# Attention plus expert layer on one Trainium2 core: a ninth shared pair of chunks, other step orders, and the output's rows copied in DRAM

## The chip, the cores and the metric

The kernel runs on one core of one Trainium2 chip. The metric is device microseconds of one execution. Before the change three runs took 1771.78 to 1775.19 us, with a median of 1773.52 us.

The engines have the names of the profile: PE is TensorE (matrix multiply), DVE is VectorE, ACT is ScalarE, POOL is GpSimd, and SP is SyncE, which here only issues DMAs.

## The reference

Eight batches of 2496 tokens with 256 features pass through an attention without softmax, and every token then goes to at most one of eight experts.

```python
scores = (1 / S) * (z @ z.T)             # z: 8 x 2496 x 64; the same z on both sides
attn = np.maximum(scores, 0.0) ** 2      # symmetric, since scores is
x = u * (attn @ v)                       # u, v: 8 x 2496 x 256
# mixture of experts over the 19968 rows of x
do_compute = x @ w_skip > 0              # the other rows go out as x
e = argmax(x @ w_gate); g = softmax(x @ w_gate)[e]
out = x + g * (relu(x @ w1[e]) @ w2[e])  # w1: 8 x 256 x 1024, w2: 8 x 1024 x 256
```

## The kernel before, in words

**Chunks and steps.** Each batch has five chunks of queries, numbered 0 to 4: four of 512 queries and a last one of 448. For each chunk the kernel walks over the keys in ten steps of 256 keys, p = 0 to 9. Keys 2p and 2p+1 (in units of 128) form step p, and p // 2 is the number of the group of 512 keys, so that group j holds the same tokens as chunk j. `steps` lists all 400 pairs (chunk, p) in the order that the table `ORDER` gives for each chunk number; chunk 0 of batch 0 goes straight through. Below, "step k" is the k-th step of a chunk in that order, from 0, and "p" is the number of the keys.

**What one step does.** PE multiplies z by z for 256 keys (`scores`, L263): six matmuls on half the array's rows, three passes of two that run side by side. ACT takes the relu from PSUM (L304) and squares it (L305) into a tile `r`. `r` is then split into a high part `ah` (a cast, L327, on ACT or DVE) and a low part `al` (a subtraction on DVE, L331), so that PE can multiply in its reduced fp32 format without losing digits. PE then accumulates v against `ah` and `al` (`attend`, L358): 12 matmuls for each half d of the features, 24 for a step (18 for p = 9), each reading 512 or 448 columns, again two side by side.

**Shared weights.** Because the weights are symmetric, the block (chunk c, key group j) is the transpose of (chunk j, key group c). The table `PAIRS` says which blocks are computed once: for a pair (c, j), chunk c computes the two steps of group j, DVE transposes `r` in blocks (`keep`, L280), and SP writes the result to a DRAM buffer `kept` (L705, four DMAs for a pair, at most four in a step). Chunk j later reads it back (`recall`, L292, four DMAs for a step) and has no scores, relu or square for those two steps. Chunk 4 has 448 queries in another layout than the others; for a recalled step of it the cast and the subtraction are each made in three pieces. Batch 0 uses only the pairs whose first chunk isn't 0.

**Which engine casts.** `on_act` puts the cast on ACT for the steps of a pair, on both sides, and for the steps listed in `EXTRA` for that chunk; the other casts are on DVE.

**Order of the work.** The order on each engine is the order of the program, written out by hand. In step k the program first issues the recall for five steps ahead, then makes the scores and weights for two steps ahead, then multiplies step k. The second half of the features (d = 1) lags: step 0 and step 8 multiply d = 0 alone, step 1 also does d = 1 of steps 0 and 1, and step 9 does d = 1 of steps 8 and 9. In step 9 the program does this, in order:

1. d = 0 of step 9;
2. the split of the next chunk's step 0 (cast and subtraction), ahead of `part` when the cast is on DVE, behind `part` when it is on ACT;
3. `part(0, ...)`: ACT copies one half of the accumulators out (L386), DVE adds the other (L388);
4. scores, relu and square of the next chunk's step 1;
5. d = 1 of steps 8 and 9;
6. `part(1, 1)`, an ACT copy that waits for the end of d = 1;
7. the cast of the next chunk's step 1, then the DVE add, then the subtraction, and then the multiplication by u (`mul`, L391).

If the next chunk's step 1 is a recalled one, its cast and subtraction come ahead of point 6 instead.

**After a chunk.** Two steps after the end come the router's matmuls (`gates`) and the first of two transposes of the rows on DVE (L395), then the second; `store` (L404) then writes the rows from the tile `xrow` with four DMAs into `xr` (in DRAM, read later by the experts), and a step later, with four more, into `out`. Each of these DMAs moves pieces of 256 bytes. After every other chunk the routing of two chunks follows on DVE: `logits` at two steps after the end, `route` and `counts` at four, `place` at six. DVE also splits the next batch's z and v as they arrive.

**Limits that matter here.** There are five `r` tiles, three each of `ah` and `al`, two of the PSUM tiles for scores, and two of the transposed tile `rt`. After the last chunk the experts run: rows are gathered from `xr` by POOL, two matrix products follow, and the results are scattered over the rows of `out` (L666).

Of the kernel before, what the change touches and what calls it, by code (L numbers as in the profile page):

```python
# [25 lines left out]

PAIRS = ((0, 1), (0, 2), (0, 3), (1, 2), (1, 3), (2, 3), (2, 4), (3, 4))
ORDER = (  # L30
# [5 lines left out]
)  # L36
EXTRA = ((8,), (3, 8), (4, 5), (6, 7), (1, 3))


C_TRI, C_REV, C_OFF, C_IDS, C_THR, C_END = 0, 128, 192, 256, 260, 270  # L40
# [7 lines left out]
def attn_moe(ctx, tc, zT, uT, v, wg, w1, w2, cst, pad, out):  # L48
# [322 lines left out]
    def finish(ci):  # L371

        b, q0, n = chunks[ci]
        t0 = b * S + q0
        xT = xTs[ci] = uts.pop(ci)

        nm = n // 32
        xrow = xp.tile([P, QC // 32, D // 4], F32, name="xrow", tag="xrow")


        e = xrow.rearrange("p a b -> p (a b)").rearrange("p (d q) -> p d q", d=2)

        def part(d, t, acc):

            if t:
                nc.scalar.copy(e[:, d, :n], acc[1][:, :n])  # L386
            else:
                nc.vector.tensor_add(e[:, d, :n], acc[0][:, :n], e[:, d, :n])  # L388

        def mul():  # L390
            nc.vector.tensor_mul(xT[:, :, :n], e[:, :, :n], xT[:, :, :n])  # L391

        def turn_rows(d):

            nc.vector.transpose(  # L395
                xrow[:, :nm, 32 * d : 32 * d + 32], xT[:, d, :n].rearrange("p (m i) -> p m i", i=32)
            )

        dsts = [xr, out]

        def store():
            dst = dsts.pop(0)
            for a in range(4):
                nc.sync.dma_start(  # L404
                    dst[t0 : t0 + n, 64 * a : 64 * a + 64].rearrange("(m i) e -> i m e", i=32),
                    xrow[32 * a : 32 * a + 32, :nm, :],
                )

        return part, mul, lambda: turn_rows(0), lambda: turn_rows(1), store
# [365 lines left out]
    for s, (ci, p) in enumerate(steps):  # L775
        b, q0, n = chunks[ci]
        k = s % NP
        step[0] = s
        ahead(s + LA + 3)
        if k == 0:  # L780
            accs[ci] = [[ps_acc.tile([P, QC], F32, name="acc", tag="acc") for _ in range(2)] for _ in range(2)]
        acc = accs[ci]
        if k < NP - 1:
            high, low = stage(s + LA)
            if k < NP - 2 or s + LA in known:
                high()
                low()
                high = low = lambda: None
            while k == NP - 3 and put_off:
                put_off.pop()()  # L790
            attend(b, n, p, 0, acc[0], *aa[s], k == 0, False)
            for t in () if k in (0, NP - 2) else (s - 1, s) if k == 1 else (s,):
                attend(b, n, steps[t][1], 1, acc[1], *aa.pop(t), t % NP == 0, False)
            rest = high, low
        else:


            part, mul, rows0, rows1, store = finish(ci)
            attend(b, n, p, 0, acc[0], *aa[s], False, True)

            high, low = rest
            if s + 1 < len(steps) and not on_act(*steps[s + 1]):
                high()
                low()
                high = low = lambda: None
            part(0, 1, acc[0])
            part(0, 0, acc[0])
            high()
            low()
            high, low = stage(s + LA)  # L810
            attend(b, n, steps[s - 1][1], 1, acc[1], *aa.pop(s - 1), False, False)
            if s + LA in known:

                high()
                low()
                high = low = lambda: None
            attend(b, n, p, 1, acc[1], *aa.pop(s), False, True)
            part(1, 1, acc[1])
            high()
            part(1, 0, acc[1])  # L820
            low()
            mul()
            accs.pop(ci)

            new.append(ci)
            if ci < NC - 1:
                after = [(rows0, 2), (rows1, 3), (store, 4), (store, 5)]
                if ci % 2 == 0:
                    gates, logits, route, counts, gate, place, put_in = routing(new)
                    after = [(gates, 2), (logits, 2), (rows0, 2), (rows1, 3), (route, 4), (counts, 4),  # L830
                             (store, 4), (gate, 5), (store, 5), (place, 6)]
                    for t in range(0, 4 * len(new), 2):
                        f = lambda put_in=put_in, t=t: put_in(t, t + 2)
                        if s + 6 + t < len(steps):
                            after.append((f, 6 + t))
                        else:
                            left.append(f)
                    new = []
                for f, k in after:
                    todo.setdefault(s + k, []).append(f)  # L840
            else:
                gates, logits, route, counts, gate, place, put_in = routing(new, False)
        for f in todo.pop(s, []):
            f()
        put_some()
# [50 lines left out]
    def add(fills, *slots):  # L896
        for k, f in slots:
            fills.setdefault(k, []).append(f)
# [4 lines left out]
    for e in range(E):  # L903
# [3 lines left out]
        for i in range(NFIX):  # L907
            fills = {}
            if e:

                add(fills, (1, rows(e, i + 3)), (3, lambda: turn_pe(pair(e, i + 1), turned(e, i + 1))))
                if e == 1 and i == 0:
                    add(fills, (0, rows(1, 2)))
                if more:
                    add(fills, (4, rows(e + 1, i)))
                if i == 0 and e + 2 < E:
                    add(fills, (6, lambda: load_ids(idts[e + 2], e + 2, 2 * NSTAT)))
                add(fills, *zip((1, 3, 5), wq[3 * i : 3 * i + 3]))
            elif i == 0:
                add(fills, (0, lambda: turn_pe(pair(0, 1), turned(0, 1))))  # L920
                add(fills, (0, gates), (0, rows0), (0, rows1), (0, store), (0, store), (1, logits), (1, route),
                    (2, counts), (2, gate), (4, end_routes), (6, end_lists))
                add(fills, *zip((0, 2), left))
            elif i == 1:
                add(fills, (1, end_counts), (3, lambda: turn_pe(pair(0, 2), turned(0, 2))), (4, rows(0, 3)), (6, rows(0, 4)))
                add(fills, *zip((1, 3, 5), wq[:3]))
            else:
                add(fills, (1, rows(1, 0)), (3, rows(0, 5)), (4, lambda: turn_pe(pair(0, 3), turned(0, 3))),
                    (5, rows(1, 1)), (6, lambda: load_ids(idts[2], 2, 2 * NSTAT)))
                add(fills, *zip((1, 2, 3, 5, 6), wq[3:]))  # L930
# [99 lines left out]
```

## Time and profile before

| | before |
|---|---|
| runs | 1771.78, 1773.52, 1775.19 us |
| the profiled execution's own time | 1774.26 us |
| its span, first to last instruction | 1772.5 us |
| TensorE clock granted | 0.998 |
| busy: PE, DVE, ACT, POOL | 1751.5, 1196.0, 1159.2, 491.4 us |
| end of the attention (last `mul`) | 1276.2 us |
| DMA bytes | 267.47 MB in 403766 packets, 205859 of them under 512 bytes |

The profile is of one execution; its time and its span differ by 1.8 us, and the execution lies 0.7 us above the median of the three runs. Busy shares are averages over two stages: the attention up to 1276 us, and the experts after it. The busy time of PE is modelled: a matmul that overlaps the one before it is counted as busy, and short waits can hide in it. They show in the distance between the starts of matmuls, which the timeline gives.

### The profile page before, as it was taken

To read this page: it belongs to the slowest core of one execution; us is meant where nothing else is said; L and a number is where in the kernel's file an instruction comes from. 1 tells how busy PE (TensorE), PEld (TensorE's weight loads), DVE (VectorE), ACT (ScalarE), POOL (GpSimd) and SP (SyncE) were. 2 spreads that over 40 slices of the span, in tenths; PEclk is the share of its full clock that TensorE was granted. 3 is DMA by queue.
4 is the path that set the end of the run, shared out by engine and by line. 5 is a ranking of instruction groups with operands and counts; after the bars stand their busy time and mean duration, and the time that the engine had idled before them with its cause. 6 is when DMAs were issued, how large, how long until landed. Compare 5 with 4: busy or idle time off the path is not lost. (4 is left out here: it accounts for less than half of the span.)

```text
span 1772.5 us, 40706 instructions
## 1 busy us (share of the span) xinstructions
PE 1751.5 (99%) x15844; PEld 1571.7 (89%) x15844; DVE 1196.0 (67%) x2113; ACT 1159.2 (65%) x1499; POOL 491.4 (28%) x483
## 2 busy tenths in 40 slices
PE   8999999999999999999999999999999999999998
PEld 6879888988888898888889888888899999999998
DVE  6878877887887787788778778867753333343332
ACT  8878877887788788778778877877533323333321
POOL 1102212211220221221122022112355546635721
PEclk9999999999999999999999999999999999999999
DMA  5576689478858947885794789579543323323210
GB/s 191 126 186 147 162 212 226 103 197 219 175 141 203 226 108 195 219 201 134 185 219 114 195 211 206 119 193 217 146 112 88 82 80 110 92 54 93 87 38 27
DMA packets 403766, 267.47 MB, mean 151 GB/s; under 512 B 205859, under 2 KB 334117, under 8 KB 403440
## 3 DMA queue, kind: packets, MB, share of 16 engines
q1 hardware_dynamic: 389440, 240.47, 55.6%
q0 software_dynamic: 13712, 22.99, 4.6%
q8 instruction: 142, 2.33, 0.6%
q14 instruction: 184, 1.51, 0.3%
q10 hardware_dynamic: 288, 0.17, 0.0%
HBM read 145.80 MB, written 118.39 MB: 149 GB/s over the span
## 5 line engine op out<-in xcount | busy, mean ns | idle before, releaser
L358 PE MATMUL acc<-ah,vh 64*128 64x512 f32 (+1 forms) x3120 | 654.6, 383 | 1.2 <-DVE ah L327 0.6
L358 PE MATMUL acc<-ah,vl 64*128 64x512 f32 (+1 forms) x3120 | 638.0, 382 | 0.0
L331 DVE TENSOR_TENSOR al<-r,ah 128x1024 fp32r<-128x1024 f32 (+3 forms) x464 | 488.4, 1068 | 185.2 <-ACT ah L327 175.4
L358 PE MATMUL acc<-al,vh 64*128 64x512 f32 (+1 forms) x3120 | 506.3, 383 | 2.2 <-DVE al L331 1.6
L517 POOL DMA_INDIRECT lst<-pair,dest x160 | 197.2, 1233 | 911.7 <-DVE dest L515 875.9
L304 ACT ACTIVATE r<-ps 128x1024 f32<-128x1024 f32 (+1 forms) x278 | 279.9, 1007 | 167.7 <-PE ps L263 158.7
L358 PEld LDWEIGHTS acc<-ah,vh 64*128 64x128 f32 x3120 | 344.6, 184 | 50.7 <-ACT ah L327 3.5
L358 PEld LDWEIGHTS acc<-ah,vl 64*128 64x128 f32 x3120 | 343.3, 184 | 41.3 <-DVE vl L120 0.3
L358 PEld LDWEIGHTS acc<-al,vh 64*128 64x128 f32 x3120 | 320.5, 184 | 53.0 <-DVE al L331 11.7
L327 ACT CAST ah<-r 128x1024 fp32r<-128x1024 f32 (+3 forms) x381 | 330.6, 892 | 55.5 <-PE acc L358 35.4
L305 ACT ACTIVATE r<-r 128x1024 f32<-128x1024 f32 (+1 forms) x278 | 290.0, 1043 | 8.8
L622 ACT ACTIVATE hh<-psh 128x512 fp32r<-128x512 f32 (+1 forms) x172 | 99.1, 584 | 287.9 <-PE psh L617 249.4
L617 PE MATMUL psh<-xt,w1h 128*128 128x256 f32 (+1 forms) x1280 | 235.3, 285 | 2.0 <-ACT xt L588 1.4
L636 PE MATMUL y<-w2t,hh 128*128 128x256 f32 x1328 | 235.5, 280 | 0.0
L623 DVE SCALAR_TENSOR_TENSOR hl<-psh,hh 128x512 fp32r<-128x512 f32 (+1 forms) x172 | 113.3, 671 | 137.5 <-ACT hh L622 134.6
L636 PEld LDWEIGHTS y<-w2t,hh 128*128 128x128 f32 x1328 | 201.8, 188 | 1.0 <-issue 0.6
L617 PEld LDWEIGHTS psh<-xt,w1h 128*128 128x128 f32 x1280 | 197.4, 189 | 2.9 <-issue 2.9
L636 PE MATMUL y<-w2t,hl 128*128 128x256 f32 x664 | 184.5, 278 | 1.3 <-DVE hl L623 1.3
L617 PE MATMUL psh<-xt,w1l 128*128 128x256 f32 (+1 forms) x640 | 182.1, 285 | 0.5 <-issue 0.5
L280 DVE STREAM_TRANSPOSE rt<-r 128x512 f32<-128x512 f32 x244 | 158.3, 686 | 0.7 <-DMA kept<-rt 0.5
L636 PEld LDWEIGHTS y<-w2t,hl 128*128 128x128 f32 x664 | 124.7, 188 | 1.7 <-DVE hl L623 1.7
L666 POOL DMA_INDIRECT out<-o,idt x77 | 76.7, 996 | 171.4 <-DVE o L665 148.6
(178 smaller groups left out, 1694.9 us busy)
## 6 DMA issues: line engine op xcount, KB each, us to landing
kept<-rt SPq DMA_DIRECT2D x244, 256.0 KB, 4.7
r<-kept SPq DMA_DIRECT2D x488, 128.0 KB, 4.5
raw<-in_v SPq DMA_DIRECT2D x80, 256.0 KB, 4.4
ut<-in_uT SPq DMA_DIRECT2D x32, 512.0 KB, 4.6
xr<-xrow SPq DMA_DIRECT2D x128, 128.0 KB, 3.2
out<-xrow SPq DMA_DIRECT2D x128, 128.0 KB, 3.0
raw<-in_w SPq DMA_DIRECT2D x64, 256.0 KB, 3.7
zf<-in_zT SPq DMA_DIRECT2D x40, 256.0 KB, 4.9
```

Source lines behind the costliest of these rows:

```text
L280: nc.vector.transpose(t[:, :, 32 * k : 32 * k + 32], r[:, x, :].rearrange("p (m i) -> p m i", i=32))
L304: nc.scalar.activation(r[:, :, :n], ps[:, :, :n], AF.Relu, scale=isc)
L305: nc.scalar.activation(r[:, :, :n], r[:, :, :n], AF.Square)
L327: (nc.scalar.copy if on_act(ci, p) else nc.vector.tensor_copy)(h_, r_)
L331: nc.vector.tensor_sub(l_, r_, f32(h_))
L358: nc.tensor.matmul(acc[t][:, :n], w[h, x, dd], a[h, x, :n], start=(first and t not in halves[:m]), stop=(last and t not in halves[m + 1 :]),)
L517: put = nc.gpsimd.indirect_dma_start(out=lst, out_offset=bass.IndirectOffsetOnAxis(ap=dest[:, t : t + 1], axis=0), in_=pair[:, t, :], in_o ...
L617: nc.tensor.matmul(ps[:, j * W : (j + 1) * W], wt[:, a, o : o + P], x[:, d, :W], start=(m == 0), stop=(m == 5),)
L622: nc.scalar.activation(hh[:, : G * W], ps[:, : G * W], AF.Relu)
L623: nc.vector.scalar_tensor_tensor(hl[:, : G * W], ps[:, : G * W], 0.0, f32(hh[:, : G * W]), op0=ALU.max, op1=ALU.subtract)
L636: nc.tensor.matmul(ys[t], h[:, tt], w2t[f][:, k, :], start=(f == 0 and m == 0 and t % 2 == 0), stop=(f == NF - 1 and m == 2), skip_group_c ...
L666: put = nc.gpsimd.indirect_dma_start(out=out, out_offset=bass.IndirectOffsetOnAxis(ap=ids[:, t, 0:1], axis=0), in_=ot, in_offset=None, bou ...
```

## The change

The pair (1, 4) joins the table, in all eight batches. Chunk 1 transposes and keeps the weights of its steps p = 8 and 9, and chunk 4 recalls them for p = 2 and 3. The order of chunk 1 changes, so that the kept groups 2, 3 and 4 each have their two steps side by side and the recalled steps p = 0 and 1 come at k = 3 and k = 6. `EXTRA` changes: in chunk 1, p = 8 leaves the list (it is in a pair now); in chunk 4, p = 0, 1 and 8 are cast on ACT in place of p = 1 and 3. `store` keeps its first part. Its second part becomes one DMA from `xr` to `out`, in 64 contiguous pieces of 7 or 8 KB, issued four steps after the first part instead of one (after the last chunk: in a later slot of the first unit of expert 0).

```diff
-PAIRS = ((0, 1), (0, 2), (0, 3), (1, 2), (1, 3), (2, 3), (2, 4), (3, 4))
+PAIRS = ((0, 1), (0, 2), (0, 3), (1, 2), (1, 3), (1, 4), (2, 3), (2, 4), (3, 4))
 ORDER = (
     (0, 1, 2, 3, 8, 4, 5, 6, 7, 9),
-    (2, 3, 0, 4, 1, 5, 8, 6, 7, 9),
+    (2, 4, 5, 0, 6, 7, 1, 8, 9, 3),
     (4, 0, 1, 6, 2, 7, 3, 8, 9, 5),
     (6, 0, 2, 1, 8, 3, 9, 4, 5, 7),
     (0, 1, 2, 3, 4, 5, 6, 7, 8, 9),
 )
-EXTRA = ((8,), (3, 8), (4, 5), (6, 7), (1, 3))
+EXTRA = ((8,), (3,), (4, 5), (6, 7), (0, 1, 8))
...
-        dsts = [xr, out]
+        stored = []
 
         def store():
-            dst = dsts.pop(0)
+            if stored:
+                to, of = (t[t0 : t0 + n, :].rearrange("(p r) d -> p (r d)", p=64) for t in (out, xr))
+                nc.sync.dma_start(to, of)
+                return
+            stored.append(True)
             for a in range(4):
                 nc.sync.dma_start(
-                    dst[t0 : t0 + n, 64 * a : 64 * a + 64].rearrange("(m i) e -> i m e", i=32),
+                    xr[t0 : t0 + n, 64 * a : 64 * a + 64].rearrange("(m i) e -> i m e", i=32),
                     xrow[32 * a : 32 * a + 32, :nm, :],
                 )
...
-                after = [(rows0, 2), (rows1, 3), (store, 4), (store, 5)]
+                after = [(rows0, 2), (rows1, 3), (store, 4), (store, 8)]
...
                     after = [(gates, 2), (logits, 2), (rows0, 2), (rows1, 3), (route, 4), (counts, 4),
-                             (store, 4), (gate, 5), (store, 5), (place, 6)]
+                             (store, 4), (gate, 5), (place, 6), (store, 8)]
...
-                add(fills, (0, gates), (0, rows0), (0, rows1), (0, store), (0, store), (1, logits), (1, route),
+                add(fills, (0, gates), (0, rows0), (0, rows1), (0, store), (3, store), (1, logits), (1, route),
```

## The prediction

> **What bounds the kernel now.** I read the page first, then the windows of the five chunks of one batch, then the timelines of PE, ACT and DVE around the steps that the change touches.
>
> ```profile
> span 1772.5 us, 40706 instructions
> PE 1751.5 (99%) x15844; PEld 1571.7 (89%) x15844; DVE 1196.0 (67%) x2113; ACT 1159.2 (65%) x1499; POOL 491.4 (28%) x483
> PEclk9999999999999999999999999999999999999999
> ```
>
> PE is busy from end to end at its full clock; no other engine is near it. The windows of chunks 1 to 4 of batch 4 say whether that holds where the change is made (columns: the stretch, then busy time and count of PE, PEld, DVE, ACT and POOL, the clock, DMA share, GB/s):
>
> ```profile
> 680.38:712.72 32.34, 32.34 (x310) 26.11 (x310) 27.33 (x58) 25.71 (x30) 5.40 (x4) 1.00 0.76 187
> 712.72:744.22 31.50, 31.40 (x274) 25.32 (x272) 22.31 (x29) 25.00 (x27) 6.74 (x6) 1.00 0.88 216
> 744.22:776.26 32.04, 31.78 (x308) 26.06 (x306) 25.33 (x52) 22.58 (x28) 5.28 (x4) 1.00 0.90 220
> 776.26:803.71 27.45, 27.45 (x270) 25.72 (x268) 23.48 (x38) 21.46 (x34) 6.33 (x8) 1.00 0.66 146
> ```
>
> In chunks 1 and 4 PE is never idle by this count, so fewer matmuls mean less time, as long as the data for the others are ready. That is the question, because each removed matmul also takes away time in which ACT and DVE prepare the next step. The page cannot answer it; the distances on the timelines can.
>
> **Term 1: the scores that go.** At the turn from chunk 3 to chunk 4 of batch 4, PE's timeline reads:
>
> ```profile
> 773.13 0.62 PE L358 MATMUL acc<-al,vh 64*128 64x512 f32 x4
> 773.58 0.36 PE L263 MATMUL ps<-zh 64*128 64x448 f32 x2
> ...
> 774.19 0.36 PE L358 MATMUL acc<-ah,vh 64*128 64x448 f32 x2
> ...
> 775.00 0.57 PE L358 MATMUL acc<-al,vh 64*128 64x448 f32 x4
> 775.41 0.36 PE L263 MATMUL ps<-zh 64*128 64x448 f32 x2
> ...
> 776.02 0.36 PE L358 MATMUL acc<-ah,vh 64*128 64x448 f32 x2
> ...
> 776.82 0.37 PE L358 MATMUL acc<-al,vh 64*128 64x448 f32 x2
> ```
>
> One step's scores take 774.19 - 773.58 = 0.61 us. Chunk 4 loses them for p = 2 and 3 in all eight batches: 16 x 0.61 = 9.8 us. The Trainium skill (TensorE: Matmul & The Clock Gate, Back-to-back issue gap) gives N/2.4 + 2.5 ns between warm matmuls; an estimate from it is 189 ns a pass, 9.1 us in all, and a sum 0.7 us smaller. The trace has the duration, so 9.8 stands.
>
> **Term 2: what the lost scores covered.** The two groups of scores above, at 773.58 and 775.41, are exactly those of p = 2 and 3. They stand between the end of chunk 3 and the first use of chunk 4's step p = 1. That step is not a recalled one, so the program casts it behind the ACT copy of chunk 3's last accumulators, and that copy waits for PE. ACT, then DVE:
>
> ```profile
> 773.79 0.59 ACT L386 COPY xrow<-acc 128x512 f32<-128x512 f32 x1 [0.84 <-PE acc L358]
> 774.27 0.94 ACT L327 CAST ah<-r 128x896 fp32r<-128x896 f32 x1
> ```
>
> ```profile
> 775.25 1.09 DVE L331 TENSOR_TENSOR al<-r,ah 128x896 fp32r<-128x896 f32 x1 [0.15 <-ACT ah L327]
> ```
>
> The chain is tied to the end of chunk 3 at 773.58: copy, cast done at 775.21, subtraction done at 776.34. PE wants `ah` at 776.02 and `al` at 776.82, so today the chain is 0.48 us early. Without the two groups PE wants `ah` at 774.80 and `al` at 775.60, both 1.22 us sooner, while the chain cannot start sooner. `ah` is then 0.41 us late and `al` 0.74 us late in all. This wait is new, on the path, and comes once in each batch: 8 x 0.74 = 5.9 us. Behind it on PE stands everything; ACT and DVE merely get ahead. The low end is 0.41 (only the cast is late): 3.3 us. The high end comes from the cast of p = 0, which the change puts on ACT ahead of this copy: 0.94 us into an idle time of 0.84, so 0.10 later, 0.84 in all, 6.7 us. I take 5.9, since each link has its row.
>
> That such a chain stops PE can be seen today at the turn from chunk 0 to chunk 1, where step 2 is recalled and only one group of scores lies between. PE, then DVE:
>
> ```profile
> 680.10 0.48 PE L358 MATMUL acc<-ah,vl 64*128 64x512 f32 x2
> 680.52 0.72 PE L358 MATMUL acc<-al,vh 64*128 64x512 f32 x4
> ```
>
> ```profile
> 679.24 1.23 DVE L331 TENSOR_TENSOR al<-r,ah 128x1024 fp32r<-128x1024 f32 x1 [0.26 <-ACT ah L327]
> ```
>
> PE starts `al` at 680.52, just after the subtraction ends at 680.47, where a start at about 680.33 was due by the pace of the rest. The page's busy count does not show this 0.2 us. In the new chunk 1 the group between moves from step 3 to step 2, so this small wait stays as it is.
>
> **Term 3: the fuller DVE in chunk 1.** Four more transposes cost DVE 4 x 0.69 = 2.7 us in each chunk 1:
>
> ```profile
> L280 DVE STREAM_TRANSPOSE rt<-r 128x512 f32<-128x512 f32 x244 | 158.3, 686 | 0.7 <-DMA kept<-rt 0.5
> ...
> L327 DVE CAST ah<-r 128x1024 fp32r<-128x1024 f32 x51 | 36.6, 718 | 17.7 <-ACT r L305 17.5
> ```
>
> One cast (of p = 9 or its successor at the chunk's end) leaves DVE, 0.7 us, so its load in chunk 1 goes from 27.3 to some 29.3 of 32.3 us. That fits on average. In even batches the routing falls there too, and the order matters. DVE in batch 4, then PE:
>
> ```profile
> 691.90 1.23 DVE L331 TENSOR_TENSOR al<-r,ah 128x1024 fp32r<-128x1024 f32 x1 [2.84 <-ACT ah L327]
> 693.05 1.30 DVE L280 STREAM_TRANSPOSE rt<-r 128x512 f32<-128x512 f32 x2
> ...
> 697.69 0.69 DVE L120 TENSOR_TENSOR vl<-raw,vh 128x512 fp32r<-128x512 f32 x1
> 698.29 2.35 DVE L331 TENSOR_TENSOR al<-r,ah 128x1024 fp32r<-128x1024 f32 x2
> ```
>
> ```profile
> 687.79 0.39 PE L263 MATMUL ps<-zqh,zh 64*128 64x512 f32 x2
> ...
> 688.47 0.39 PE L358 MATMUL acc<-ah,vh 64*128 64x512 f32 x2
> ```
>
> ```profile
> 699.76 0.62 PE L358 MATMUL acc<-al,vh 64*128 64x512 f32 x4
> ```
>
> The subtraction for k = 6 is the first of the two at 698.29, done at about 699.45; PE wants it at 699.76, 0.3 us later. In the new order k = 4 has scores, so those of k = 5 at 687.79, and the subtraction, transposes and routing behind them, come one group (688.47 - 687.79 = 0.68 us) later, while PE's own date for k = 6 stays (two groups are missing before it in both orders). 0.3 - 0.68 makes a wait of about 0.35 us in batches 2, 4 and 6: 1.1 us. The low end is 0, if the 2.84 us in which DVE idled before 691.90 take it up; the high end 0.68 in four batches, 2.7 us.
>
> **Costed at nothing.** Chunk 4's ACT and DVE lose two relus, two squares and some casts, which only adds room. The recalls and the copy go through SP and the DMA rings. DMA issues with KB each and us to landing, and the windows of chunk 4's first half:
>
> ```profile
> r<-kept SPq DMA_DIRECT2D x488, 128.0 KB, 4.5
> ...
> xr<-xrow SPq DMA_DIRECT2D x128, 128.0 KB, 3.2
> out<-xrow SPq DMA_DIRECT2D x128, 128.0 KB, 3.0
> ```
>
> ```profile
> 774.00:780.00 6.00, 6.00 (x62) 5.57 (x60) 4.79 (x7) 5.91 (x8) 1.87 (x2) 1.00 1.00 224
> 780.00:786.00 6.00, 6.00 (x64) 5.55 (x62) 6.00 (x9) 4.63 (x12) 4.46 (x7) 1.00 1.00 159
> 786.00:792.00 6.00, 6.00 (x62) 5.56 (x60) 5.01 (x12) 3.42 (x6) 0.00 (x0) 1.00 1.06 257
> 792.00:798.00 6.00, 6.00 (x62) 5.46 (x62) 4.64 (x6) 4.61 (x7) 0.00 (x0) 1.00 0.30 90
> ```
>
> The rings are full until 792 and then nearly empty. Eight recalls more (1 MB, 4.7 us at 224 GB/s) make the last ones later, and the four `out` stores that go give about half back. The cover is that a recalled step is cast two steps (2 x 2.44 us, from 774.19 to 775.41 twice for one) before its matmuls. The new wait in front of the copy holds SP's queue, with recalls and puts behind it; the `xr` stores land in 3.2 us and the copy is issued four steps, some 10 us, after them, so it finds them landed. A copy inside DRAM is not in the trace: between 3.0 us (one store) and 12 us (four in a row). It matters only at the end of the attention, where POOL's first scatter must wait for the last copy. SP, then POOL:
>
> ```profile
> 1279.67 2.00 SPq L404 DMA_DIRECT2D xr<-xrow  x4
> ```
>
> ```profile
> 1295.84 0.98 POOL L666 DMA_INDIRECT out<-o,idte  x1 [0.30 <-issue]
> ```
>
> Stores landed at about 1285 and a copy of 12 us end at 1297, at worst 1 us late; I take 0.
>
> **Sum.** -9.8 + 5.9 + 1.1 = -2.8 us against the profiled execution's 1774.26 us (span 1772.5 and 1.8 around it): 1771.5. That execution lies 0.7 us above the median of the runs, 1773.52, so the median after is 1770.7. With the ends of the terms the change lies between -6.5 and -0.4: 1767.0 to 1773.1. Runs of this kernel can tell 0.2%, 3.5 us, from no change.
>
> **The rivals.** *The saving goes through*: PE does not stop at p = 1, because what I call a chain is looser than the one execution shows. -9.8 + 1.1 gives 1764.8. For it speaks that PE counts no idle time in chunk 4; against it that the copy waited for PE and each link follows within 0.1 us. *Slower, by late recalls*: six recalled steps in a row meet full rings. If 4.7 us of delay and a landing that grows from 4.5 to 6 us exceed the cover of 4.9 by 1.3 us, eight batches pay 10.4 and the result is 1781.1. It decides from 0.35 us a batch (no gain) and from 0.8 us (slower by 0.2%). Against it: the `out` stores leave the rings, and the first two recalls come when no others are due. *Relief of the rings*: fewer small packets end the waits in chunks 2 and 3, where PE lacks 0.10 and 0.26 us; seven batches make 2.5, and 1768.2. The Trainium skill (DMA: Bandwidth & Descriptors, Specifications) asks for at least 512 bytes a piece for full rate, which the old stores miss. The trace does not bear that out here: their 128 KB land in 3.0 us, those of the recalls in 4.5.
>
> **How the numbers follow.** The forecast has 0.58: 0.40 within 0.2%, 0.16 faster, 0.02 slower. The saving that goes through has 0.17 and the relief 0.10, both faster. Late recalls have 0.15: 0.12 slower, 0.03 the same. That makes 0.43, 0.43 and 0.14. The range reaches down past the first rival, 1764.0, and up to 1776.5, into the mild part of late recalls.
>
> **What would show it.** After: no scores for p = 2 and 3 in chunk 4; PE idle for about 0.4 and then 0.3 us at the second step of chunk 4 in all batches, released by ACT's cast (L327) and DVE's subtraction (L331); a small wait at k = 6 of chunk 1 in even batches. I am wrong if PE runs through that second step, or if it waits for `r<-kept` in the middle of chunk 4.

## The result, and the profile after

The kernel after takes 1802.95 us (median of four runs, 1800.52 to 1805.44), the kernel before, run beside it, 1774.30 us (median of four). The ratio is 1.0167, with a 95% interval of 1.0154 to 1.0179: 29 us slower, where 3 us less were forecast. Two later sets of runs repeat it, with 1795.35 us against 1772.13 (1.0138, 1.0116 to 1.0159) and 1790.91 against 1773.01 (1.0111, 1.0094 to 1.0127). So from set to set the kernel after differs by up to 12 us and the kernel before by 3: a few us between runs of different sets say little. The profiled execution is the one of 1800.52 us. First its page:

```profile
span 1798.7 us, 40622 instructions
PE 1758.3 (98%) x15748; PEld 1534.9 (85%) x15748; DVE 1198.5 (67%) x2145; ACT 1161.4 (65%) x1531; POOL 501.3 (28%) x483
```

There are 96 matmuls fewer (16 groups of six), as the change says, the granted clock is 0.997, and yet PE is idle for 40 us instead of 21. The attention's last `mul` comes at 1301.5 us instead of 1276.2. So 25 of the profiled execution's 26 us are lost before the experts. The windows of chunks 1 to 4 of batch 4 in the kernel after (columns as before):

```profile
696.29:728.22 31.93, 31.59 (x302) 25.25 (x300) 27.75 (x59) 25.89 (x30) 5.59 (x4) 1.00 0.79 197
728.22:759.52 31.30, 31.20 (x272) 25.14 (x270) 22.31 (x28) 24.81 (x27) 6.55 (x6) 1.00 0.86 224
759.52:791.57 32.05, 31.50 (x300) 25.21 (x296) 24.77 (x50) 23.24 (x30) 6.20 (x4) 1.00 0.83 195
791.57:823.33 31.76, 28.99 (x264) 24.67 (x264) 22.71 (x39) 19.86 (x35) 7.33 (x8) 1.00 0.76 179
```

Chunks 1 to 3 are within half a microsecond of before. Chunk 4, which had 27.45 us without idle time, has 31.76 us, of which PE is busy for 28.99. So the loss is in chunk 4. What it waits for is in the list of waits (us in total, times, longest), first of before, then of after:

```profile
ACT ah L327 <- DMA r<-kept: 6.7, 7, 3.4
```

```profile
ACT ah L327 <- DMA r<-kept: 58.0, 31, 4.0
```

ACT's casts wait for recalled tiles 58.0 us in place of 6.7. One chunk shows how that reaches PE. ACT's timeline in chunk 4 of batch 4, after:

```profile
795.54 1.13 ACT L327 CAST ah<-r 128x384 fp32r<-128x384 f32 x3 [3.95 <-DMA r<-kept]
798.71 1.13 ACT L327 CAST ah<-r 128x384 fp32r<-128x384 f32 x3 [2.04 <-DMA r<-kept]
...
802.19 1.13 ACT L327 CAST ah<-r 128x384 fp32r<-128x384 f32 x3 [1.82 <-DMA r<-kept]
...
805.43 1.13 ACT L327 CAST ah<-r 128x384 fp32r<-128x384 f32 x3 [1.60 <-DMA r<-kept]
...
808.86 1.12 ACT L327 CAST ah<-r 128x384 fp32r<-128x384 f32 x3 [1.78 <-DMA r<-kept]
...
810.41 0.91 ACT L304 ACTIVATE r<-ps 128x896 f32<-128x896 f32 x1
...
813.71 0.91 ACT L304 ACTIVATE r<-ps 128x896 f32<-128x896 f32 x1
```

and PE's in the same stretch, the lines that carry a wait and the last scores of p = 8:

```profile
799.89 0.47 PE L358 MATMUL acc<-ah,vh 64*128 64x448 f32 x2 [0.21 <-ACT ah L327]
801.86 0.68 PE L358 MATMUL acc<-al,vh 64*128 64x448 f32 x4 [0.89 <-DVE al L331]
...
806.74 0.36 PE L263 MATMUL ps<-zh,zl 64*128 64x448 f32 x2
...
816.32 0.47 PE L358 MATMUL acc<-ah,vh 64*128 64x448 f32 x2 [1.19 <-DVE ah L327]
```

Five recalled tiles in a row (p = 3 to 7) come after ACT is ready for them. One of them, p = 4, stops PE directly, twice: by its cast at 799.89 and by its subtraction at 801.86. The second stop has another cause beside the late recall: DVE takes 2.55 us for that subtraction (from 799.26), where the next recalled tile's takes 1.18, and POOL's casts of z (L242) run beside it. At the usual pace it would have ended at 800.5, before PE asked for it at about 800.8. The largest stop, at 816, is named for DVE's cast, a step that is not recalled at all. It goes back to the same cause: the scores of p = 8 are done at 807.1, but their relu runs at 810.41, because ACT works in program order and stands until 808.86 at the cast of the last recalled tile. The relu of p = 9 follows at 813.71, behind p = 8's square and its own cast, and everything behind that is late.

To add this up I take PE's time from the first matmul of a step (d = 0) to that of the next, kernel after minus kernel before, summed over the eight batches. Idle marks alone would give too little: at 790.58 (below) the mark says 0.31 us, the starts say 0.46. In chunk 4:

| step k | 0 | 1 | 2 | 3 | 4 | 5 | 6 | 7 | 8 | 9 |
|---|---|---|---|---|---|---|---|---|---|---|
| us | -1.1 | +3.3 | 0.0 | +0.8 | +6.8 | +1.8 | +1.8 | +0.5 | +8.0 | +4.7 |

Steps 0 and 1 sum to +2.2, steps 2 to 9 to +24.4. By batch, chunk 4 changes by +4.8, +2.9, +6.1, +1.1, +4.9, +1.7, +4.9 and +0.1. The last batch, for which no next batch is loaded, loses nothing, but that alone proves little: the even batches (0, 2, 4, 6) lose 4.8 to 6.1 us and the odd ones 0.1 to 2.9, and when the kernel after was run again two odd batches with their loads (3 and 5) lost only 0.3 each. In the odd batches chunk 4 is 1.4 us longer already in the kernel before (29.0 against 27.6 us from its first matmul to the next chunk's), with the router's matmuls in it; that this extra time is what saves them is not shown. All else of the attention is -1.4. The same sums (chunk 4, steps 0 and 1 | steps 2 to 9, against the kernel before) stand beside the experiments; they are of the one profiled execution of each run.

### The profile page after: what moved, and what is told of

It is laid out like the page before. It is cut to its first block, busy times and chain, and to the rows that moved or that the text cites. A ratio compares the mean times of both kernels' runs of the same rounds, so it can differ in the third digit from the quotient of the medians.

```text
span 1798.7 us, 40622 instructions
## 1 busy us (share of the span) xinstructions
PE 1758.3 (98%) x15748; PEld 1534.9 (85%) x15748; DVE 1198.5 (67%) x2145; ACT 1161.4 (65%) x1531; POOL 501.3 (28%) x483
## 4 chain that ended last, share of the span: by engine, by line
PE 69%; DMA 12%; DVE 7%; ACT 7%; issue 2%; SPq 2%; POOL 0%; DVEq 0%; POOLq 0%; ACTq 0%
PE acc L358 38%; PE psh L621 11%; PE y L640 11%; PE ps L263 8%; DMA r<-kept 6%; DVE al L331 3%; ACT ah L327 2%; DMA out<-o,idt 2%; ACT r L305 2%; DMA out<-xr 2%; ACT r L304 2%; SPq L292 1%; DVE rt L280 1%; PE pst L590 1%; DMA zf<-in_zT 1%
## 5 line engine op out<-in xcount | busy, mean ns | idle before, releaser
L358 PE MATMUL acc<-ah,vh 64*128 64x512 f32 (+1 forms) x3120 | 636.9, 385 | 12.3 <-DVE ah L327 6.3
L358 PE MATMUL acc<-ah,vl 64*128 64x512 f32 (+1 forms) x3120 | 619.1, 382 | 0.0
L358 PE MATMUL acc<-al,vh 64*128 64x512 f32 (+1 forms) x3120 | 494.4, 385 | 10.5 <-DVE al L331 9.4
L327 ACT CAST ah<-r 128x1024 fp32r<-128x1024 f32 (+3 forms) x445 | 364.5, 847 | 107.0 <-DMA r<-kept 58.0
L358 PEld LDWEIGHTS acc<-ah,vh 64*128 64x128 f32 x3120 | 318.8, 184 | 78.0 <-ACT ah L327 15.8
L358 PEld LDWEIGHTS acc<-al,vh 64*128 64x128 f32 x3120 | 300.5, 184 | 78.1 <-DVE al L331 30.4
L358 PEld LDWEIGHTS acc<-ah,vl 64*128 64x128 f32 x3120 | 319.1, 184 | 48.1 <-DVE vl L120 0.3
L304 ACT ACTIVATE r<-ps 128x1024 f32<-128x1024 f32 (+1 forms) x262 | 265.3, 1013 | 145.2 <-PE ps L263 136.3
L305 ACT ACTIVATE r<-r 128x1024 f32<-128x1024 f32 (+1 forms) x262 | 274.8, 1049 | 8.3
L280 DVE STREAM_TRANSPOSE rt<-r 128x512 f32<-128x512 f32 x276 | 179.0, 686 | 0.4 <-DMA kept<-rt 0.4
```

The source lines that it names most:

```text
L280: nc.vector.transpose(t[:, :, 32 * k : 32 * k + 32], r[:, x, :].rearrange("p (m i) -> p m i", i=32))
L304: nc.scalar.activation(r[:, :, :n], ps[:, :, :n], AF.Relu, scale=isc)
L305: nc.scalar.activation(r[:, :, :n], r[:, :, :n], AF.Square)
L327: (nc.scalar.copy if on_act(ci, p) else nc.vector.tensor_copy)(h_, r_)
L358: nc.tensor.matmul(acc[t][:, :n], w[h, x, dd], a[h, x, :n], start=(first and t not in halves[:m]), stop=(last and t not in halves[m + 1 :]),)
```

## Experiments

**First set: which part of the change does it?** The runs of a set were made together, each set with its own runs of the kernel before; the number in brackets behind a time is the ratio to it, with its 95% interval. Kernel before: 1772.51 us. The kernel after is not in this set. Theory A is the copy inside DRAM, theory B the eight more recalls, theory C ACT's new cast of p = 8.

The copy alone, in the kernel before (in outline):

```diff
 def store():
-    dst = dsts.pop(0)     # four DMAs from xrow, to xr, then to out
+    # second time: one DMA from xr to out; slots (store, 4), (store, 8)
```

> The kernel before with only the new second part of store: one copy in DRAM from xr to out, at its new place. Eight pairs, old orders, old casts. Theory A (the copy makes the recalls of chunk 4 late: it stands in SP's queue and in the rings right ahead of them, takes 6.5 us to land where a store took 3.0): slower than before by 3 to 12 us, with ACT waiting for r<-kept in chunk 4 for more than the 6.7 us of before. Theory B (the eight more recalls of the ninth pair make them late, and the copy is harmless): within 2 us of before, 1772 to 1776.

1771.97 us, ratio 0.9995 (0.9986 to 1.0005). The page has 124067 packets under 512 bytes, 81792 fewer than before, and the time is the same. Theory A falls as the only cause.

The pair alone, with the old store (in outline, against the kernel after):

```diff
-                nc.sync.dma_start(to, of)           # xr to out
+            dst = dsts.pop(0)                       # [xr, out], from xrow
-(store, 8)
+(store, 5)
```

> The changed kernel with the old store: four more DMAs from xrow to out, one step after the first four. Ninth pair, new orders, new casts. Theory A: the late recalls go, the 24 us lost in steps 3 to 9 of chunk 4 with them, and what is left is the sum of the prediction, 1769 to 1776. Theory B: still slower by 15 us or more, 1789 or above. Both half: around 1785.

1789.79 us (1.0084, 1.0065 to 1.0104), with four runs as far apart as 1783.97 and 1798.32; the profiled one is the slowest. Chunk 4 there: +2.2 | +21.2, ACT's wait for recalls 67.4 us. The loss needs no copy.

The kernel after with p = 8, and then with p = 1, cast on DVE:

```diff
-EXTRA = ((8,), (3,), (4, 5), (6, 7), (0, 1, 8))
+EXTRA = ((8,), (3,), (4, 5), (6, 7), (0, 1))     # e3
+EXTRA = ((8,), (3,), (4, 5), (6, 7), (0, 8))     # e4
```

> The changed kernel with the cast of p = 8 in chunk 4 on DVE again. Theory C (the 12.7 us lost at steps 8 and 9 of chunk 4 come from this cast, which loads ACT there): 1790 to 1795. Theories A and B (they come from ACT standing at the late cast of p = 7, with the relu of p = 8 queued behind it): no more than 3 us better, 1800 to 1804, as the relu is late all the same.

1787.48 us (1.0081, 1.0064 to 1.0098); +2.2 | +18.7. The time lies below both expected ranges, which were reckoned from the kernel after in its first set. The sums decide: step 8 falls from 8.0 to 3.4 us (6.2 is the least that the kernel after has there in three sets), and of the steps before it 11.2 us stay of 11.7. So the cast makes the late recalls dearer, but is not their cause. C falls as the main cause.

> The changed kernel with the cast of p = 1 in chunk 4 on DVE, so that it no longer stands behind ACT's copy of the accumulators. If the wait at step 1 of chunk 4 is on the path as the second term of the prediction has it (now 7.1 us in eight batches by the starts of PE): 1794 to 1798. Rival: the late recalls end last anyway and swallow it, so that the time gained at step 1 is lost at step 4: 1801 to 1804, and only the place of the wait moves.

1789.94 us (1.0102, 1.0085 to 1.0119); +0.3 | +18.5; this time, too, lies below both ranges. The stop that the prediction's second term foresaw shrinks by 1.8 us (its `ah` part goes, its `al` part grows); the loss in steps 2 to 9 is there without it.

**Second set: are the recalls late, and by what?** Kernel before: 1772.13 us.

The kernel after again, unchanged, as the mark of this set:

> The kernel after, unchanged, as the mark for the other three of this call. Expected near 1800 us (ratio about 1.016); if the landing of the copy inside DRAM differs on this chip (6.5 us in the first profile, about 5.2 us in the earlier experiments), a few us less.

1795.35 us; +2.3 | +23.5.

The new recalls of chunk 4 without their DMAs (with other weights other tokens go to the experts, so the attention's sums count here more than the total):

```diff
 def recall(ci, p):
     r = r_tile()
+    if ci % NQ == 4 and p in (2, 3):
+        nc.gpsimd.memset(r, 0.0)
+        return r
```

> Chunk 4's two new recalled tiles are filled with zeros by POOL in place of the eight recall DMAs, so the kernel leaves the weights of those two blocks out. Matmuls, casts and subtractions stay. Late recalls (the rings and SP's queue in chunk 4 hold too much): PE's lost time at steps 3 to 9 of chunk 4, about 24 us over eight batches in the kernel after, falls to under 6 us, and the attention ends within 5 us of the kernel before; the stop of about 0.9 us at chunk 4's second step stays. ACT's place in the order (the late cast of p = 8): the loss at steps 8 and 9, some 12 us, stays with or without the DMAs, and the end comes some 12 to 15 us after that of the kernel before.

1772.28 us; +2.4 | +0.4, and over the whole attention -0.9 us by the starts. Every matmul, cast and subtraction of the kernel after is there; without the 1 MB a batch the 24 us are gone, those at steps 8 and 9 too. That decides for late recalls and against ACT's order as a cause of its own.

The next batch's loads three steps later:

```diff
-(load_v, 7, 4, 2), (load_z, 2, 4, 3), (load_v, 8, 4, 4), (load_z, 3, 4, 5), (load_v, 9, 4, 6), (load_z, 4, 4, 7)
+(load_v, 7, 4, 5), (load_z, 2, 4, 6), (load_v, 8, 4, 7), (load_z, 3, 4, 8), (load_v, 9, 4, 9), (load_z, 4, 4, 10)
```

> The next batch's loads of v and z that fall into chunk 4 (256 KB pieces) are issued three steps later, behind the burst of recalls. Late recalls by rings that are full until two thirds of the chunk: the recalls land in time, ACT's wait for recalled tiles falls from some 58 us to under 15 us, and the time falls by 10 us or more, to 1775 to 1790. If the recalls are late by SP's own queue and the limited number of DMAs in flight rather than by bytes, the gain is the same, since the loads stand in that queue too. ACT's place in the order: no more than 3 us less than the kernel after.

1781.56 us (1.0053, 1.0036 to 1.0070); +2.2 | +1.6. The late recalls are cured with all the recalls in place. But steps 0 and 1 of chunk 0 now cost 7 us, a new loss (below). ACT's wait for recalls is still 28.2 us, where 15 at most was expected: much of such waiting costs PE nothing.

Chunk 4 in another order:

```diff
-    (0, 1, 2, 3, 4, 5, 6, 7, 8, 9),
+    (0, 2, 1, 3, 4, 8, 5, 6, 9, 7),
```

> Only chunk 4's order of steps changes: its recalled steps are spread among the fresh ones (0 2 1 3 4 8 5 6 9 7 in place of 0 to 9), so that recalls are due over seven steps in place of six in a row, and the chunk's second step is a recalled one. Late recalls: with more time between the dates the loss at steps 3 to 9 shrinks by half or more, and the stop at the second step (7 us over eight batches) goes, since its cast no longer stands behind the accumulators' copy: 1765 to 1785. If a recall in second place comes too late itself (issued two steps before chunk 4), a new stop there by ACT waiting for a recalled tile takes its place. ACT's place in the order: little change, 1790 to 1800.

1775.89 us (1.0024, 1.0012 to 1.0036); -4.8 | +8.5. As expected, less than half of the loss is left and the stop at the second step is gone. The even batches' chunk 4 is 0.4 to 0.6 us shorter than before (batches 0, 2, 4, 6), the odd ones' 1.0 to 1.8 longer.

**Third set: bytes or queue, and what a cure costs.** Kernel before: 1772.50 us.

The kernel after with chunk 4's loads (`load_v` 7 to 9, `load_z` 2 to 4) from POOL's queue (in outline):

```diff
-        nc.sync.dma_start(t, src)
+        (q or nc.sync).dma_start(t, src)     # q = nc.gpsimd for b > 0 and g > 6
-        nc.sync.dma_start(zf, zT[b, :, j * QC : (j + 1) * QC])
+        (nc.gpsimd if b and j > 1 else nc.sync).dma_start(zf, zT[b, :, j * QC : (j + 1) * QC])
```

> The kernel after with the next batch's six loads of chunk 4 issued by POOL's queue at the same places in the program; the bytes are the same and at about the same time. Bytes (the DMA engines are full for two thirds of chunk 4, and the order in which the queues are served decides little): no gain, 1788 to 1800. SP's queue (recalls stand behind loads there, with a limited number of DMAs in flight): recalls are issued earlier, the waits of ACT for recalled tiles fall below 20 us, and the time falls to 1770 to 1782.

1796.45 us (1.0133, 1.0116 to 1.0150); +2.2 | +22.5. So it is not the loads' place in SP's queue: the recalls no longer stand behind them there, and PE loses as much (ACT still waits 42.4 us for recalls, 49.3 in the kernel after of the second set). The loads themselves, in that run's DMA issues:

```profile
raw<-in_v SPq DMA_DIRECT2D x59, 256.0 KB, 4.3
raw<-in_v POOLq DMA_DIRECT2D x21, 256.0 KB, 7.1
```

The Trainium skill (Trainium Kernel Development and Optimization, Key Constraints) says that DMAs from the SP, ACT and POOL queues share the same 16 DMA engines and interleave, so that a second issuer saves issue time only. The run agrees, by 1796.45 us against 1795.35 of the kernel after in the second set.

Order 0 2 1 3 to 9, and loads two steps later (the last two together), with the copy and with the old store; and those loads, without the order, in the kernel before (the two lines of `jobs` are put into one here and below):

```diff
-    (0, 1, 2, 3, 4, 5, 6, 7, 8, 9),
+    (0, 2, 1, 3, 4, 5, 6, 7, 8, 9),
-(load_v, 7, 4, 2), (load_z, 2, 4, 3), (load_v, 8, 4, 4), (load_z, 3, 4, 5), (load_v, 9, 4, 6), (load_z, 4, 4, 7)
+(load_v, 7, 4, 4), (load_z, 2, 4, 5), (load_v, 8, 4, 6), (load_z, 3, 4, 7), (load_v, 9, 4, 8), (load_z, 4, 4, 8)
```

> The kernel after with two edits: chunk 4 goes 0 2 1 3 to 9, so that a recalled step is second, and the next batch's loads come two steps later (the last two together). If the loss of the kernel after is the stop at the second step (7.1 us in all) plus late recalls (some 23 us) and nothing else, both go, and the sum is -9.8 + 2 = about -8 us against the kernel before: 1764, up to 1768 if splits of z and v that come late cost PE something at the end of chunk 4. If the second recalled step in a row of places 1, 3, 4, 5 meets full rings all the same, ACT waits for recalled tiles there and the time is 1772 to 1782.

> As the run with the swap and the later loads, but with the store of the kernel before (the rows written twice from the tile, one step apart). If the copy inside DRAM holds up recalls behind it in SP's queue in the kernel after, its absence gives up to 3 us more here: 1761 to 1765. If it is harmless, as it was alone in the kernel before (ratio 0.9995): within 2 us of the run with the copy.

> The kernel before with the next batch's loads of chunk 4 two steps later. The kernel before has only four recalled steps there, and its ACT waits for recalled tiles 6.7 us in all, none of which reaches PE: no change, within 2 us of the kernel before. If the later loads alone give several us, then what the other runs gain by them is not the cure of late recalls.

e10: 1775.82 us (1.0022, 1.0012 to 1.0032); -4.9 | +2.3. e11: 1782.44 us (1.0058, 1.0042 to 1.0075); -4.9 | +6.1. e12: 1779.81 us (1.0039, 1.0024 to 1.0053); 0 | +0.5. None came out as the sum has it (e10 has the figure of its second expectation, but not its cause: recalls cost it 2.3 us at most). e12 tells why: the later loads cost the kernel before itself 7.2 us at the start of chunk 0. DVE and then PE there, at the turn to batch 3 in e12:

```profile
486.04 0.70 DVE L120 TENSOR_TENSOR vl<-raw,vh 128x512 fp32r<-128x512 f32 x1 [1.43 <-ACT vh L119]
486.65 0.69 DVE L109 TENSOR_TENSOR zl<-zf,zh 128x512 fp32r<-128x512 f32 x1
...
488.04 1.23 DVE L331 TENSOR_TENSOR al<-r,ah 128x1024 fp32r<-128x1024 f32 x1
489.19 0.62 DVE L388 TENSOR_TENSOR xrow<-acc,xrow 128x448 f32<-128x448 f32 x1
```

```profile
488.79 0.39 PE L358 MATMUL acc<-ah,vh 64*128 64x512 f32 x1
489.86 0.50 PE L358 MATMUL acc<-ah,vh 64*128 64x512 f32 x1 [0.68 <-DVE xrow L388]
```

Two splits in step 8 push DVE's reading of the old accumulators behind PE's wish to reuse them, once a batch. The next set tests that: its e15 differs from e10 in the splits alone, and the 7.7 us that e10 loses at steps 0 and 1 of chunk 0 are gone there (-0.3).

**Fourth set: the cure without its cost, and the copy's share.** Kernel before: 1773.01 us.

The pair with the old store (the edit of the first set) and the kernel after, side by side:

> The ninth pair with the store of the kernel before, now in one call with the kernel after. If the copy inside DRAM worsens the late recalls (it stands in SP's queue among them, 512 KB read and written): 4 to 8 us less than the kernel after. If it relieves the rings (pieces of 8 KB in place of 256 bytes): 3 to 8 us more. Within 2 us: it plays no part.

> The kernel after, unchanged, as the mark of this call: 1795 to 1800 us.

e13: 1788.86 us (1.0099, 1.0084 to 1.0115); +2.3 | +13.7. e14: 1790.91 us (1.0111, 1.0094 to 1.0127); +2.3 | +19.2. The intervals overlap: what the copy adds to the kernel after can't be told from nothing here. In e10 and e11 the copy was 6.6 us better than the old store. That difference was not taken apart, and stays open.

The loads of e10, their splits a step earlier (e15), and the spread order with them and p = 5 on ACT (e16):

```diff
-(load_v, 7, 4, 2), (load_z, 2, 4, 3), (load_v, 8, 4, 4), (load_z, 3, 4, 5), (load_v, 9, 4, 6), (load_z, 4, 4, 7)
+(load_v, 7, 4, 3), (load_z, 2, 4, 4), (load_v, 8, 4, 5), (load_z, 3, 4, 6), (load_v, 9, 4, 7), (load_z, 4, 4, 7)
...
-    later(s0 + c * NB + 2 * k - 7, 7, load, b + 1, j, nc.vector)
+    m = 5 if c == 4 else 7
+    later(s0 + c * NB + 2 * k - m, m, load, b + 1, j, nc.vector)
...
-    (0, 1, 2, 3, 4, 5, 6, 7, 8, 9),
+    (0, 2, 1, 3, 4, 5, 6, 7, 8, 9),          # e15
+    (0, 2, 1, 3, 4, 8, 5, 6, 9, 7),          # e16, with EXTRA[4] = (0, 1, 5, 8)
```

> As the run with the swapped order and the later loads, with the loads at the same steps of chunk 4 (0, 1, 2, 3, 4, 4), but their splits one step earlier (3, 4, 5, 6, 7, 7), so that none stands in step 8 ahead of DVE's copy of the accumulators. If the 7 us at the start of chunk 0 came from the split in step 8, they go: 1764 to 1768, below the kernel before. If a split now waits for its load and holds ACT: 1770 to 1776. If the stop at the start of chunk 0 has another cause: 1774 to 1777 as before.

1765.27 us, ratio 0.9955 (0.9941 to 0.9968): faster than both kernels, and in the expected range. Chunk 4: -4.9 | +0.1; the attention -8.2 us. The windows of e15's chunk 4 of batch 4, in stretches of 6 us that begin as far ahead of the turn as the prediction's:

```profile
769.03:775.03 6.00, 6.00 (x62) 5.52 (x60) 5.35 (x10) 5.20 (x10) 3.19 (x3) 1.00 0.98 208
775.03:781.03 6.00, 6.00 (x62) 5.55 (x60) 6.00 (x13) 3.78 (x11) 5.05 (x7) 1.00 1.08 246
781.03:787.03 6.00, 6.00 (x62) 5.57 (x60) 3.93 (x8) 3.00 (x7) 0.42 (x1) 1.00 0.94 235
787.03:793.03 6.00, 6.00 (x62) 5.49 (x60) 3.47 (x5) 5.94 (x8) 0.00 (x0) 1.00 0.63 216
```

and the same stretches of the kernel after:

```profile
789.31:795.31 6.00, 5.64 (x54) 4.59 (x52) 4.13 (x7) 2.27 (x5) 1.86 (x2) 1.00 0.73 177
795.31:801.31 6.00, 5.44 (x52) 4.38 (x48) 3.97 (x8) 2.78 (x7) 3.48 (x5) 1.00 1.06 240
801.31:807.31 6.00, 5.40 (x50) 4.69 (x52) 5.18 (x11) 3.30 (x8) 1.98 (x3) 1.00 0.98 203
807.31:813.31 6.00, 6.00 (x59) 5.02 (x56) 2.38 (x5) 4.39 (x8) 0.00 (x0) 1.00 1.05 267
```

The DMA share is the second to last column; a packet counts in the stretch in which it starts. In e15 the engines are full for 18 us (769 to 787) and PE does not stop. In the kernel after they are full as well. The 0.73 of its first stretch leaves out the packets of the copy, which started before it: the trace records the copy as 16 packets of 32 KB (not as the 64 pieces of the program), and in this turn they held the engines for some 3 us each. Counted by the packets' own spans, the engines are 0.9 to 1.1 busy from 788 to 803. So full engines are not the difference; the order is. In e15 two of the six loads are issued before the chunk's last recall (at 772.06 and 775.38), in the kernel after four (their rows stand below).

> As the run with the spread order (0 2 1 3 4 8 5 6 9 7), with the later loads and earlier splits, and p = 5 cast on ACT in place of DVE. In that run the even batches gained 1.2 us each and the odd ones, whose routing fills DVE in chunk 4, lost 1 to 1.7. If that loss is DVE's load, the cast taken off it gives most back: 1762 to 1768. If it is ACT's wait for recalled tiles in full rings, the later loads give it back too, to the same figure; if neither, 1772 to 1776.

1772.83 us (1.0003, 0.9994 to 1.0012): even batches as in e8, odd ones +0.9 to +1.4 still, though ACT waits only 3.6 us for recalls in all. That is the last of the three cases: neither the cast taken off DVE nor the later loads give the odd batches' loss back. What PE waits for there is still DVE; why the cast didn't help was not followed up. PE's waits in chunk 4 of batch 3:

```profile
633.63 0.68 PE L358 MATMUL acc<-al,vh 64*128 64x448 f32 x4 [0.41 <-DVE al L331]
...
641.09 0.68 PE L358 MATMUL acc<-al,vh 64*128 64x448 f32 x4 [0.26 <-DVE al L331]
```

**Fifth set: whose gain is it?** Kernel before: 1771.51 us. The loads and splits of e15, without its order, in the kernel before (e17) and in the kernel after (e18):

```diff
-(load_v, 7, 4, 2), (load_z, 2, 4, 3), (load_v, 8, 4, 4), (load_z, 3, 4, 5), (load_v, 9, 4, 6), (load_z, 4, 4, 7)
+(load_v, 7, 4, 3), (load_z, 2, 4, 4), (load_v, 8, 4, 5), (load_z, 3, 4, 6), (load_v, 9, 4, 7), (load_z, 4, 4, 7)
...
-    later(s0 + c * NB + 2 * k - 7, 7, load, b + 1, j, nc.vector)
+    m = 5 if c == 4 else 7
+    later(s0 + c * NB + 2 * k - m, m, load, b + 1, j, nc.vector)
```

> The kernel before with the loads and splits of chunk 4 placed as in the best run (loads at steps 0, 1, 2, 3, 4, 4, splits at 3, 4, 5, 6, 7, 7). If the best run's 8 us belong to the ninth pair: no change, within 2 us of the kernel before. If they belong to the moved loads: 1765 to 1768.

1772.55 us (1.0011, 1.0001 to 1.0020); 0.0 | 0.0. The gain of e15 is the pair's and not the loads'.

> The kernel after with the same placement and its own order 0 to 9 in chunk 4. Late recalls cured, the stop at the second step left: PE's starts give -9.8 + 7.1 + 2 = about -1 us against the kernel before, 1771 to 1773. If some recalls are still late without the swap (the recalls begin one step earlier there than here): 1775 to 1780.

1779.14 us (1.0038, 1.0026 to 1.0051); +2.2 | +9.1, of the last 8.5 at steps 8 and 9. The second expectation holds: moving the loads alone leaves the last recalls late, so the swapped order (e15) is needed too. With it the recalls start one step earlier; that this is how it helps the late steps is likely, but no run takes it apart.

## Why the prediction was wrong, point by point

**Term 1, scores: right.** Where no stop hides it, the starts give -4.97 us at the end of chunk 3 and -4.87 at step 0 of chunk 4 (e15): 9.8 us, as forecast. The section of the Trainium skill that the prediction cites there gives its formula for an isolated matmul; here one pass takes a third of 0.61 us, 203 ns, against the 189 of the formula.

**Term 2, the stop at chunk 4's second step: the mechanism right, the size low.** In every batch it came, link by link. Batch 4 of the kernel after, on PE, ACT and DVE:

```profile
788.45 0.62 PE L358 MATMUL acc<-al,vh 64*128 64x512 f32 x4
788.90 0.36 PE L358 MATMUL acc<-ah,vh 64*128 64x448 f32 x2
...
789.71 0.56 PE L358 MATMUL acc<-al,vh 64*128 64x448 f32 x4
790.58 0.47 PE L358 MATMUL acc<-ah,vh 64*128 64x448 f32 x2 [0.31 <-ACT ah L327]
...
791.71 0.67 PE L358 MATMUL acc<-al,vh 64*128 64x448 f32 x4
792.22 0.37 PE L358 MATMUL acc<-ah,vh 64*128 64x448 f32 x2
```

```profile
789.11 0.59 ACT L386 COPY xrow<-acc 128x512 f32<-128x512 f32 x1
789.59 2.00 ACT L327 CAST ah<-r 128x896 fp32r<-128x896 f32 x4
```

```profile
790.56 1.09 DVE L331 TENSOR_TENSOR al<-r,ah 128x896 fp32r<-128x896 f32 x1
```

Copy, cast and subtraction start 0.21, 0.69 and 1.66 us after the end of chunk 3 at 788.90; the forecast had 0.21, 0.69 and 1.67. PE wanted `ah` at 788.90 + 1.22 = 790.12 and got it 0.46 us late (0.41 forecast). It came to the first `al` matmul at 791.71, 0.79 after 790.92 (0.74 forecast). What was missing is the restart: that group takes 0.51 us to the next start instead of 0.41. That makes 0.89 us in this batch, and 7.1 in all (the +2.2 above, plus the 4.9 of scores that left step 0) instead of 5.9.

**Term 3, the wait at step 6 of chunk 1: right in place, low in size.** It stands in batches 2, 4 and 6 and nowhere else. Batch 4:

```profile
714.93 0.73 PE L358 MATMUL acc<-al,vh 64*128 64x512 f32 x4 [0.34 <-DVE al L331]
```

By the starts it is 0.61, 0.61 and 0.58 us, 1.8 in all against 1.1.

**Sum of the three.** -9.8 + 7.1 + 1.8 = -0.9 us. The run without the new recalls' DMAs has -0.9 for the attention; that they agree to a tenth is in part chance, since its term 3 is 2.1 us and it has small changes elsewhere.

**The step that failed** stands in "costed at nothing": that the recalls are covered by the two steps between a recalled tile's cast and its matmuls, 4.9 us. In place of nothing, late recalls cost 24.4 us in steps 2 to 9 of chunk 4. I had set the 4.7 us that the extra megabyte takes against that cover as if each recall met it afresh. But the delay is handed on: six recalled steps in a row, each served behind the one before and behind the next batch's loads, and no free stretch in between. SP's issues in the kernel after (start, duration with its waits; each group is one recall):

```profile
785.54 1.44 SPq L404 DMA_DIRECT2D out<-xr  x1
787.08 1.95 SPq L292 DMA_DIRECT2D r<-kept  x4
789.07 0.42 SPq L95 DMA_DIRECT2D raw<-in_v  x1
789.59 4.56 SPq L292 DMA_DIRECT2D r<-kept  x4
794.52 0.35 SPq L103 DMA_DIRECT2D zf<-in_zT  x1
794.97 2.46 SPq L292 DMA_DIRECT2D r<-kept  x4
797.67 0.35 SPq L95 DMA_DIRECT2D raw<-in_v  x1
798.12 3.50 SPq L292 DMA_DIRECT2D r<-kept  x4
801.66 0.43 SPq L103 DMA_DIRECT2D zf<-in_zT  x1
802.19 2.10 SPq L292 DMA_DIRECT2D r<-kept  x4
```

SP's waits for DMAs in flight, from the list of SP's own waits in the kernel after, are part of it:

```profile
SPq L292 <- DMA r<-kept: 15.1, 43, 1.3
SPq L292 <- DMA raw<-in_v: 12.5, 17, 1.3
SPq L292 <- DMA out<-xr: 10.0, 6, 2.6
```

A recall is not issued until an earlier transfer has landed, be it a recall, a load or the copy, and the semaphores in the trace tell which: SP's DMAs use eight of them in turn, so each waits for the transfer eight places before it in SP's queue, and no more than eight of SP's are in flight. The group at 789.59 takes 4.56 us to issue for that reason: its third DMA stands 2.6 us for the copy of 785.54, eight places before it, which lands at 793.28. The landings of the recalls themselves hardly grew (4.8 us median over the run, 4.5 before; in this turn 5.4 and 5.1), those of the loads of v did (6.0 us, 4.4 before). The last recall of this chunk ends its issue at 804.3, and ACT can start its cast at 808.86. The runs show that the recalls' 1 MB (e6) and the loads' time (e7, e15) decide. For the engines' rate as the limit speak that they are full from 788 to 803 with no more than eight of SP's transfers in flight, and that e9, which takes the loads out of SP's eight places, gained nothing. No run changes the number in flight, so the two are not fully separated.

**The rival of late recalls** named the mechanism and got 0.15 and 10.4 us; it cost 24.4. Its price left out what is queued behind a waiting instruction on ACT: 12.8 of the 24.4 us arise at steps 8 and 9, whose relus stand behind the late cast. My argument against it, that the `out` stores leave the rings, was worth nothing: the copy moves the same bytes (e1: 267.42 MB, before: 267.47). The point of doubt that I named last, a wait for `r<-kept` in the middle of chunk 4, is what came. The rival in which PE runs through the second step came too, but only where the order was changed: e15's 1765.27 us beside its 1764.8. That the two figures are so near is luck, for e15 moves the loads and splits as well. The relief of the rings did not show alone (e1). The Trainium skill's rule of 512 bytes a piece (DMA: Bandwidth & Descriptors, Specifications) made no difference there; e11's time above e10's goes the way of the rule, but was not traced to it.

**The last copy** delays nothing that counts: from the attention's end to the end of the execution it is 499.0 us after and 498.1 before.

## What to carry to other kernels

When a change adds transfers to a stretch where the DMA engines are already full, don't hold one transfer's delay against one cover: write down issue, landing and due date of each in turn, since the backlog is handed on until a free stretch. Price a late transfer by what its waiting engine has queued behind it in program order, not by the instruction that waits. And move the transfers that nobody needs soon behind the urgent ones, but not so far that their own work lands on the turn to the next tile.

## What the runs showed of the hardware

Full DMA engines are not themselves a loss: e15 holds a share of 0.94 to 1.08 for 18 us in the turn shown, without a stop of PE. POOL's queue bought no time for the loads (7.1 us to landing for those in chunk 4). A copy of 512 KB from DRAM to DRAM, which the trace records as 16 packets of 32 KB, lands in a median of 6.5 us in the kernel after, between the two bounds taken, one old store (3.0) and four in a row (12). And a stop of PE is longer than its idle mark: 0.46 us by the starts at a mark of 0.31, and the group that ends the stop takes 0.10 us longer than its equals. DVE slows down beside POOL: of the 96 subtractions of 128x384 in the kernel after, six took over 0.8 us where the others take 0.51 to 0.78 (median of all 0.55), and all six ran beside one of POOL's casts of z (L242), of the other 90 only one. In e15 seven are as slow, and chunk 4 loses nothing by them.
